# Opening stage of a one-core attention and gated-MLP kernel: last keys of the first step copied within SBUF, weights for the key bound fetched in two transfers on SP, and three pieces of work put elsewhere

## Chip, cores and metric

The kernel runs on one core of a Trainium2 chip. The metric is the device time of one execution in microseconds (us), the median of three runs of the kernel before: 1417.37, from 1417.25 to 1418.29.

## What is computed

The input x is 2048 x 512. A gate weighs two branches, an attention of 32 heads (16 columns each) and a gated MLP of width 1792:

```python
g = sigmoid(sum(x * gate_w, axis=-1))
q, k, v = split(x @ wqkv)               # 32 heads of 16
a = softmax(q @ k.T / 4) @ v @ wo       # each head over 2048 keys
b = (silu(x @ w1) * (x @ w3)) @ w2
out = g * a + (1 - g) * b
```

## The kernel before

Every fp32 product is made from three matmuls: a value is split into a high part (H, h, `hi`) and a low part (L, l, `lo`), and high by high, low by high and high by low are summed in PSUM.

**The opening stage** is written out by hand and ends where the first score matmul starts. It works on x in four blocks of 512 rows (0 to 3), and on V in tiles of 128 rows:

- `load_x(b)` (L116 to L120, on SP's queue) fetches a block. `transpose_x(b)` (L149): PE transposes it (L157), ACT copies the high part out of PSUM (xH, L160), DVE subtracts the low part (xL, L161).
- `project_qk(0, b)` (L176) makes queries and keys of the first eight heads for a block: 24 matmuls (L183), then ACT copies `hi` (L187), DVE subtracts `lo` (L188), and `store_qk` (L174, SP) writes them to four tensors in HBM, `kH_d`, `kL_d`, `qH_d`, `qL_d`. Inside the one of block 0, block 1 is transposed.
- `load_v` (L194) fetches V's weights in four pieces of 256 KB (L198, SP) that POOL splits (L200 and L201). They share fetch buffers with each other, so a fetch waits for the split of the one ahead. `project_v(t)` sums a tile of V (L97, L98, L99) in one of three PSUM banks, and ACT copies it out (L212).
- The scores have a bound that lets the kernel skip the search for row maxima. `squares` (L220) squares the query and key weights (ACT L223, sums on DVE L224), eight pieces in all. The first two are those that are projected with anyway; the six others come in six transfers that ACT issues (`load_w`, L124). `x_squares(b)` (L165, ACT) sums the squares of x's rows. `bound` (L226) takes their maxima (DVE L228, PE L231 and L232, DVE L233 to L235) and writes a flag (L236).
- `guard_rows` (L238) makes two rows per head that stand beside the queries and are subtracted in the score matmul (PE L241, DVE L242 to L246), and stores them in `m_d` (L248, SP, 256 KB each).
- `load_q` (L264), `load_k` (L257) and `load_guard` (L269) fetch from HBM what the first score step needs: `Qt` and `Kt`, 50 rows for each of two heads. The last quarter of the keys, those of block 3, is fetched after `project_qk(0, 3)` has stored it, by SP for the first head of the pair and by ACT for the second.
- `x_gate(b)` (L169, DVE) sums the gate's products; after block 3 the gate is finished (L385 to L388). `load_weights` (L323) fetches the first chunk of weights for the filling matmuls, split on POOL.
- `row_maxima` (L278) reads the flag on every engine (L280) and branches (L281). With these inputs the branch's body is skipped.

V tiles 7, 8 and 9 are summed on PE ahead of the branch, and copied out by DVE behind it (L397).

**The main loop** has 1024 units: a score matmul (L768), an exponential on ACT (L772) and a product with V (L756), with half-array matmuls of the projections and of the MLP between them. An order written out as a table sets what fills which unit. The next step's queries and keys are fetched after the seventh unit.

**What sets the order.** Each engine runs its instructions in the order in which they are written. SP and ACT issue the transfers used here. A transfer reports its landing on one of eight completion counters (DMAHW0 to DMAHW7), which are taken in turn, over all queues together. Before a transfer is issued, the one before it on its counter has landed. Behind a skipped branch, SP waits for each counter and adds what the body would have added, and the first score matmul waits for all eight.

Of the kernel before, what the change touches and what calls it, by code (L numbers as in the profile page):

```python
# [8 lines left out]
F32 = mybir.dt.float32  # L9
# [8 lines left out]
P = 128  # L18
S = 2048
D = 512  # L20
F = 1792
H = 32
DH = 16
NB = S // 512
NT = S // P
ND = D // P
# [8 lines left out]
def gated_mix_kernel(ctx: ExitStack, tc: tile.TileContext, x, wqkv, wo, w1, w3, w2, gate_w, out):  # L35
# [18 lines left out]
    nc = tc.nc  # L54
# [13 lines left out]
    sqp = ph1.enter_context(tc.tile_pool(name="sqp", bufs=1))  # L68

    QD = [[dram.tile([D, S], F32, name=f"{n}{p}_d") for p in "HL"] for n in "qk"]  # L70
# [40 lines left out]
    Kt = [qkp.tile([P, S], F32R, name=f"Kt{i}") for i in range(2)]  # L111
# [3 lines left out]
    def load_x(b):  # L115
        xn[b] = p1.tile([P, 4, D], F32, name="xn", bufs=2)  # L116
        src = x[512 * b:512 * b + 512, :].rearrange("(t p) d -> p t d", p=P)
        for t in range(0, 4, 1 if b < 2 else 4):
            e = t + (1 if b < 2 else 4)
            nc.sync.dma_start(xn[b][:, t:e, :], src[:, t:e, :])  # L120

    def load_w(c, tile=None, e=nc.sync):
        w = tile if tile is not None else slot("fr", F32, (P, ND, P))
        e.dma_start(w, wqkv[:, c:c + P].rearrange("(k p) n -> p k n", p=P))  # L124
        return w

    def split_w(w):
# [21 lines left out]
    def transpose_x(b):  # L149
        xH[b] = xp.tile([P, ND, 512], F32R, name=f"xH{b}")  # L150
        xL[b] = xp.tile([P, ND, 512], F32R, name=f"xL{b}")
        parts = ((0, 1, bank()), (1, 1, bank()), (2, 2, psum2()))
        for t in range(4):
            for k0, n, ps in parts:
                for k in range(n):
                    o = ps[:, P * t:P * t + P] if n == 1 else ps[:, k, P * t:P * t + P]
                    nc.tensor.transpose(o, xn[b][:, t, P * (k0 + k):P * (k0 + k) + P], ident)  # L157
        for k0, n, ps in parts:
            ps = ps if n == 2 else ps[:, None, :]
            nc.scalar.activation(xH[b][:, k0:k0 + n, :], ps, AF.Copy)  # L160
            nc.vector.tensor_sub(xL[b][:, k0:k0 + n, :], ps, xH[b][:, k0:k0 + n, :])  # L161

    def x_squares(b):
        for t in range(4):
            nc.scalar.activation(slot("sg", F32), xn[b][:, t, :], AF.Square, accum_out=x2[:, 4 * b + t:4 * b + t + 1])  # L165

    def x_gate(b):
        for t in range(4):
            nc.vector.scalar_tensor_tensor(slot("hx", F32), xn[b][:, t, :], 1.0, gw, op0=OP.mult, op1=OP.mult,  # L169
                                           accum_out=z[:, 4 * b + t:4 * b + t + 1])  # L170
# [2 lines left out]
        for t, d in zip((hi, lo), QD[i]):  # L173
            nc.sync.dma_start(d[P * c:P * c + P, 512 * b:512 * b + 512], t.bitcast(F32) if t.dtype == F32R else t)  # L174

    def project_qk(c, b, w, between=None):  # L176
        ps = psum2()
        for i in range(2):
            if i and between:
                between()  # L180
            for n, (h, xs) in enumerate(((0, xH), (0, xL), (1, xH))):
                for k in range(ND):
                    nc.tensor.matmul(ps[:, i, :], w[i][h][:, k, :], xs[b][:, k, :], start=n == k == 0,  # L183
                                     stop=n == 2 and k == ND - 1)
        hi = p1.tile([P, 2, 512], F32R, name="hi", bufs=2)
        lo = p1.tile([P, 2, 512], F32R, name="lo", bufs=2)
        nc.scalar.activation(hi, ps, AF.Copy)  # L187
        nc.vector.tensor_sub(lo, ps, hi)  # L188
        for i in (1, 0):
            store_qk(i, c, b, hi[:, i, :], lo[:, i, :])  # L190

    wv = []

    def load_v():  # L194
        for k in range(ND):
            n = "13"[k % 2]
            r = slot("fr", F32)
            nc.sync.dma_start(r, wqkv[P * k:P * k + P, 2 * D:3 * D])  # L198
            vh, vl = slot("fh" + n), slot("fl" + n)
            nc.gpsimd.tensor_copy(vh, r)  # L200
            nc.gpsimd.tensor_sub(vl, r, vh)  # L201
            wv.append((vh, vl))

    def sums_v(t):
        ps = bank()
# [5 lines left out]
    def project_v(t):  # L211
        nc.scalar.activation(*sums_v(t), AF.Copy)  # L212
# [7 lines left out]
    def squares(w, n):  # L220

        sq = slot("raw", F32, (P, ND, P))
        nc.scalar.activation(sq, w, AF.Square)  # L223
        nc.vector.tensor_reduce(rs[:, n, :], sq.rearrange("p k (h d) -> p h k d", d=DH), axis=AX.XY, op=OP.add)  # L224
# [13 lines left out]
    def guard_rows():  # L238
        ps = bank()
        one = V[0:1, 0, :, DH:DH + 1].rearrange("p h o -> p (h o)")  # L240
        nc.tensor.matmul(ps[0:H, 0:1], one, top[:, 2:3], start=True, stop=True)  # L241
        nc.vector.tensor_copy(mm, ps[0:H, 0:1])  # L242
        ones = V[0:H, :, :, DH:DH + 1].rearrange("p t h o -> p (t h o)")
        r = [slot("sg", F32R, (H, 512)) for _ in range(2)]
        nc.vector.tensor_scalar(r[0], ones, mm, None, op0=OP.mult)
        nc.vector.tensor_scalar(r[1], r[0], -1.0, mm, op0=OP.mult, op1=OP.add)  # L246
        for a in range(2):
            nc.sync.dma_start(M_d[:, a, :].rearrange("h (j t) -> h j t", t=512),  # L248
                              r[a][:].bitcast(F32)[:, None, :].to_broadcast([H, 4, 512]))

    def load_k(j, i, b0=0, b1=NB, e=(nc.sync, nc.sync)):
        c = slice(512 * b0, 512 * b1)
        for h in range(2):
            r = 64 * h
            s = slice(DH * (2 * j + h), DH * (2 * j + h) + DH)
            for o, ks in enumerate((0, 0, 1)):
                e[h].dma_start(Kt[i][r + DH * o:r + DH * o + DH, c].bitcast(F32), QD[1][ks][s, c])  # L257

    def load_q(j, half, i):
        for h in range(2):  # L260
            r = 64 * h
            s = slice(DH * (2 * j + h), DH * (2 * j + h) + DH)
            for o, qs in enumerate((0, 1, 0)):
                nc.sync.dma_start(Qt[i][r + DH * o:r + DH * o + DH, :].bitcast(F32),  # L264
                                  QD[0][qs][s, 1024 * half:1024 * half + 1024])

    def load_guard(j, half, i):
        for h in range(2):
            nc.sync.dma_start(Qt[i][64 * h + 48:64 * h + 50, :].bitcast(F32),  # L269
                              M_d[2 * j + h, :, 1024 * half:1024 * half + 1024])  # L270
# [48 lines left out]
    def load_weights(chunk):  # L319
        out = []  # L320
        for n, w in zip("13", chunk["src"]):
            r = slot("fr", F32, (P, ND, P))
            nc.sync.dma_start(r, w.rearrange("(k p) n -> p k n", p=P))  # L323
            if chunk["first"]:
                wh = slot("raw", F32R, (P, ND, P))
                wl = slot("raw" if n == "1" else "gw", F32R, (P, ND, P))
                split(wh, wl, r)
            else:
                wh = slot("fh" + n, F32R, (P, ND, P))
                wl = slot("fl" + n, F32R, (P, ND, P))  # L330
                splits.append((issued + 6, lambda a=(wh, wl, r): split(*a)))
            out.append((wh, wl))
        chunk["w"] = out

    chunks = [dict(src=(wqkv[:, P * c:P * c + P], wqkv[:, D + P * c:D + P * c + P]), first=c == 1)
              for c in range(1, ND)]
# [11 lines left out]
    wq = [split_w(w) for w in w0]  # L348
    for i in range(2):
        squares(w0[i], ND * i)  # L350
    ws = [(ND * i + c, load_w(i * D + P * c, sqp.tile([P, ND, P], F32, name=f"s{i}{c}"), nc.scalar))
          for i in range(2) for c in range(1, ND)]
    load_v()
    project_qk(0, 0, wq, lambda: transpose_x(1))
    x_squares(0)
    x_gate(0)
    load_x(2)
    project_qk(0, 1, wq)
    x_squares(1)
    x_gate(1)  # L360
    load_x(3)
    project_v(0)
    for n, w in ws[:ND - 1]:
        squares(w, n)
    project_v(1)
    for n, w in ws[ND - 1:]:
        squares(w, n)
    project_v(2)
    transpose_x(2)
    fill_k()  # L370
    project_v(3)
    x_squares(2)
    x_squares(3)
    project_qk(0, 2, wq)
    project_v(4)
    bound()
    transpose_x(3)
    guard_rows()
    x_gate(2)
    project_v(5)  # L380
    load_q(0, 0, 0)
    load_k(0, 0, 0, 3)
    load_guard(0, 0, 0)
    x_gate(3)
    nc.scalar.activation(g, z, AF.Exp, scale=-1.0)  # L385
    nc.vector.tensor_scalar(g, g, 1.0, None, op0=OP.add)
    nc.vector.reciprocal(g, g)
    nc.vector.tensor_scalar(omg, g, -1.0, 1.0, op0=OP.mult, op1=OP.add)  # L388
    load_weights(chunks[0])
    project_qk(0, 3, wq)  # L390
    load_k(0, 0, 3, NB, (nc.sync, nc.scalar))
    project_v(6)

    last_v = [sums_v(t) for t in range(7, EARLY_V)]
    row_maxima()
    for to, src in last_v:
        nc.vector.tensor_copy(to, src)  # L397
    ph1.close()
# [423 lines left out]
    k = ND - 1  # L822
# [14 lines left out]
    for t in range(NT // 2, NT):  # L837
        n, r = divmod(t - NT // 2, 2)
# [20 lines left out]
    for b in (2, 3):  # L859
        o, r = orr[b - 2]  # L860
# [34 lines left out]
```

## Time and profile before

| | us |
|---|---|
| median of three runs | 1417.37 |
| lowest and highest run | 1417.25, 1418.29 |
| the profiled execution | 1417.44 |
| its span, from the first to the last instruction | 1415.7 |
| PE (TensorE) busy | 1400.2 (99%) |
| ACT (ScalarE) busy | 1028.9 (73%) |
| DVE (VectorE) busy | 487.0 (34%) |
| POOL (GpSimd) busy | 319.5 (23%) |

The mean granted TensorE clock is 0.996 of full speed. The span leaves out 1.74 us around the first and the last instruction. PE's row counts matmuls; PEld is its weight loads, which run beside them. Times in timelines count from the start of the span. A row of DMA issues (SPq, ACTq) gives the time from the first issue's start to the last one's end, waits between them included.

### The profile page before, as it was taken

The page shows a single profiled execution, that of the slowest core. Times are in us where ns is not written, and L with a number is a line of the kernel's source. Part 1 is how long each engine was busy: PE and PEld are TensorE (multiplying, and loading weights), DVE is VectorE, ACT ScalarE, POOL GpSimd, SP SyncE. Part 2 cuts the span into 40 slices and gives each one's busy share as a digit, 9 for nine tenths or more (in the row PEclk, how much of TensorE's full clock was granted, in tenths as well). Part 3 has the DMA queues.
Part 4 walks back from the last instruction along what each step waited for, and adds up shares of the span by engine and source line. Part 5 has one row for each costly group of instructions (what it writes and reads, how often), then busy time and mean ns, then how long its engine had stood idle before and what let it go on. Part 6 is the DMA issues. An engine that isn't in the chain of part 4 may idle for free.

```text
span 1415.7 us, 29018 instructions
## 1 busy us (share of the span) xinstructions
PE 1400.2 (99%) x11471; PEld 833.0 (59%) x11471; DVE 487.0 (34%) x1079; ACT 1028.9 (73%) x1147; POOL 319.5 (23%) x356
## 2 busy tenths in 40 slices
PE   8999999999999999999999999999999999999998
PEld 6765565665655656656556556566555555555556
DVE  5501111254545455454555545541010110110113
ACT  4457776777777777777777777777688788878880
POOL 4201444211100110011011021643324332232240
PEclk9999999999999999999999999999999999999999
DMA  7623454533312333223232522544433342354434
GB/s 241 145 49 64 135 136 131 122 92 75 76 53 63 105 77 76 63 80 83 57 77 71 116 78 66 147 105 114 121 91 94 102 107 62 76 133 110 97 125 177
DMA packets 112863, 141.44 MB, mean 100 GB/s; under 512 B 16496, under 2 KB 70768, under 8 KB 109744
## 3 DMA queue, kind: packets, MB, share of 16 engines
q1 hardware_dynamic: 107312, 134.04, 38.1%
q10 hardware_dynamic: 5408, 5.47, 1.2%
q8 instruction: 92, 1.51, 0.5%
q14 instruction: 51, 0.42, 0.1%
HBM read 90.70 MB, written 48.76 MB: 99 GB/s over the span
## 4 chain that ended last, share of the span: by engine, by line
PE 94%; ACT 0%; DVE 0%; issue 0%; ACTq 0%
PE acc L756 33%; PE f L414 27%; PE S L768 19%; PE f L544 11%; PE f L630 1%; PE f L423 1%; PE f L97 0%; PE f L98 0%; PE f L99 0%; PE S L99 0%; PE S L98 0%; PE S L97 0%; ACT p L772 0%; PE acc L99 0%; PE acc L98 0%; PE acc L97 0%
## 5 line engine op out<-in xcount | busy, mean ns | idle before, releaser
L772 ACT ACTIVATE p<-S 128x1024 f32<-128x1024 f32 x1024 | 967.1, 1025 | 313.9 <-PE S L768 305.8
L756 PE MATMUL acc<-p,V 128*17 128x512 f32 x4096 | 472.1, 594 | 0.0
L768 PE MATMUL S<-Qt,Kt 50*128 50x512 f32 x2048 | 408.8, 410 | 0.9 <-PEq L281 0.6
L768 PEld LDWEIGHTS S<-Qt,Kt 50*128 50x128 f32 x2048 | 184.7, 184 | 175.8 <-issue 77.8
L756 PEld LDWEIGHTS acc<-p,V 128*17 128x17 f32 x4096 | 103.6, 97 | 276.4 <-issue 274.6
L457 DVE RECIPROCAL sg<-sg 128x64 f32<-128x64 f32 x448 | 209.5, 517 | 51.8 <-issue 49.7
L414 PE MATMUL f<-xL,fh 64*128 64x512 f32 x1024 | 206.0, 391 | 0.0
L414 PE MATMUL f<-xH,fh 64*128 64x512 f32 x1024 | 205.9, 390 | 0.0
L414 PE MATMUL f<-xH,fl 64*128 64x512 f32 x1024 | 205.5, 390 | 0.0
L316 POOL CAST fh<-fr 128x512 fp32r<-128x512 f32 x32 | 20.0, 626 | 436.5 <-DMA fr<-in_B_w_dram 425.7
L414 PEld LDWEIGHTS f<-xH,fh 64*128 64x128 f32 x1024 | 99.7, 186 | 21.8 <-DVE tick L729 0.4
L414 PEld LDWEIGHTS f<-xL,fh 64*128 64x128 f32 x1024 | 100.1, 187 | 20.9
L414 PEld LDWEIGHTS f<-xH,fl 64*128 64x128 f32 x1024 | 99.0, 184 | 20.2
L729 DVE MEMSET tick<- 1x1 f32 x196 | 11.6, 59 | 283.1 <-PE f L544 157.2
L544 PE MATMUL f<-xH,fl 64*128 64x512 f32 x208 | 61.8, 390 | 0.0
L544 PE MATMUL f<-xL,fh 64*128 64x512 f32 x208 | 60.9, 391 | 0.0
L544 PE MATMUL f<-xH,fh 64*128 64x512 f32 x208 | 59.8, 391 | 0.0
L449 DVE COPY gs<-f 128x512 f32<-128x512 f32 x56 | 38.7, 691 | 60.8 <-PE f L414 59.5
L544 PE MATMUL f<-xH,raw 64*128 64x512 f32 x192 | 56.1, 391 | 0.0
L737 DVE COPY u<-acc 128x512 f32<-128x512 f32 x32 | 22.1, 691 | 96.6 <-PE acc L756 93.6
L455 DVE TENSOR_SCALAR sg<-sg 128x512 f32<-128x512 f32 x56 | 26.2, 467 | 82.4 <-ACT sg L454 80.3
L563 DVE SCALAR_TENSOR_TENSOR y<-f,omg,y 128x512 f32<-128x512 f32 x32 | 24.0, 751 | 78.2 <-PE f L544 78.2
(231 smaller groups left out, 1366.2 us busy)
## 6 DMA issues: line engine op xcount, KB each, us to landing
Kt<-kH_d SPq DMA_DIRECT2D x124, 128.0 KB
h_d<-sg SPq DMA_DIRECT2D x56, 256.0 KB
sg<-h_d SPq DMA_DIRECT2D x43, 256.0 KB
fr<-in_B_w_dram SPq DMA_DIRECT2D x42, 256.0 KB
Qt<-qH_d SPq DMA_DIRECT2D x128, 64.0 KB
Kt<-kL_d SPq DMA_DIRECT2D x62, 128.0 KB
Qt<-qL_d SPq DMA_DIRECT2D x64, 64.0 KB
b_d<-y SPq DMA_DIRECT2D x16, 256.0 KB
```

The lines of the kernel that those rows point to most:

```text
L316: nc.gpsimd.tensor_copy(hi, src)
L414: return nc.tensor.matmul(ps, w[i == 2][r, k, :], (xL if i == 1 else xH)[b][r, k, :], start=n == 0 and not second, stop=n == 3 * ND - 1 an ...
L423: return nc.tensor.matmul(ps, (xL if i == 2 else xH)[b][r, k, o:o + P], wv[k][i == 1][r, :], start=n == 0 and not second, stop=n == 3 * ND ...
L449: nc.vector.tensor_copy(gs, ps)
L455: small.append(lambda: nc.vector.tensor_scalar(sg, sg, 1.0, None, op0=OP.add))
L457: small.append(lambda q=q: nc.vector.reciprocal(sg[:, q:q + 64], sg[:, q:q + 64]))
L544: ins = nc.tensor.matmul(ps, hs[t][q][i == 2][r, P * o:P * o + P], (w2L if i == 1 else w2H)[q][r, o, :], start=n == 0 and not second, stop ...
L563: nc.vector.scalar_tensor_tensor(y, ps, omg[:, t:t + 1], y, op0=OP.mult, op1=OP.add)
L737: nc.vector.tensor_copy(u, acc)
L756: nc.tensor.matmul(acc[r:r + DH + 1, :], V[:, k, 2 * j + h, :], p[:, h, :], start=k == 0, stop=k == NT - 1)
L768: nc.tensor.matmul(ps[:, h, :], Kt[i][r:r + 50, P * k:P * k + P], Qt[i][r:r + 50, t:t + 512], start=True, stop=True)
L772: nc.scalar.activation(p, ps, AF.Exp, scale=SCALE)
```

## The change

It has four parts:

- The six transfers for the bound, on ACT's queue, become two of 768 KB on SP's: `sk` (the key weights) between the second and the third of V's weights, `sq` (the query weights) after `load_x(2)`. The squares of `sk` stand after `project_v(0)`, those of `sq` after `project_v(3)`.
- The keys of block 3 are no longer fetched from HBM. `last_keys` copies them from `hi` and `lo` in SBUF into `Kt`, six transfers of 32 KB, issued by SP and ACT by turns, ahead of the stores of `hi` and `lo`.
- `load_q` and `load_k` for the first three blocks stand ahead of `guard_rows`.
- `x_gate(3)` and the gate's end stand behind `project_qk(0, 3)` and `project_v(6)`, and the first `load_weights` behind the branch.

The main loop is the same, its transfers too, but that the counters which they take are turned by four.

SP's instructions where V's weights are fetched, as a piece of the difference (fr are the fetch buffers, gw the gate's weights):

```order
 L138 DMA gw<-in_gate_w_dram 128x512
-L198 DMA fr<-in_A_wqkv_dram 128x512 x4
+L200 DMA fr<-in_A_wqkv_dram 128x512 x2
+L124 DMA sk<-in_A_wqkv_dram 128x4x384
+L200 DMA fr<-in_A_wqkv_dram 128x512 x2
 L174 DMA kH_d<-hi 128x512
 L174 DMA kL_d<-lo 128x512
```

One transfer of 768 KB now stands between the second and the third piece of V's weights.

ACT's instructions from V tile 2 to the `hi` of block 2, of before:

```order
L212 ACTIVATE V<-f 128x32x16
L160 ACTIVATE xH_427<-f 128x512 x2
L160 ACTIVATE xH_427<-S 128x1024
L212 ACTIVATE V<-f 128x32x16
L165 ACTIVATE sg,x_106<-xn 128x512 x8
L187 ACTIVATE hi<-S 128x1024
```

And of the change:

```order
L160 ACTIVATE xH_410<-f 128x512 x2
L160 ACTIVATE xH_410<-S 128x1024
L216 ACTIVATE V<-f 128x32x16
L227 ACTIVATE raw<-sq 128x512 x3
L165 ACTIVATE sg,x_106<-xn 128x512 x8
L187 ACTIVATE hi<-S 128x1024
```

Three squares of `sq` now stand between V tile 3 and the eight squares of x.

SP's instructions of the change around the guard stores and the keys of block 3, with the semaphores that each waits for (m_d are the guard rows, the counters' names end in _49):

```order
L267 DMA Kt_110<-kL_d 16x1536 [waits DMAHW5_49,Pool_49]
L252 DMA m_d<-sg 32x4x512 [waits DMAHW6_49,DVE_49]
L252 DMA m_d<-sg 32x4x512 [waits DMAHW7_49,DVE_49]
L279 DMA Qt_108<-m_d 2x1024 [waits DMAHW7_49,DMAHW6_49,DMAHW0_49]
L279 DMA Qt_108<-m_d 2x1024 [waits DMAHW1_49]
L259 DMA Kt_110<-hi 16x512 [waits DMAHW2_49,Activation_49]
L259 DMA Kt_110<-hi 16x512 [waits DMAHW3_49]
L259 DMA Kt_110<-lo 16x512 [waits DMAHW4_49,DVE_49]
L174 DMA kH_d<-hi 128x512 [waits DMAHW5_49]
L174 DMA kL_d<-lo 128x512
L174 DMA qH_d<-hi 128x512
L174 DMA qL_d<-lo 128x512 [waits DMAHW0_49]
```

And ACT's of the change at the same place:

```order
L187 ACTIVATE hi<-S 128x1024 [waits DMAHW6_49,DMAHW0_49,PE_49]
L259 DMA Kt_110<-hi 16x512 [waits DMAHW6_49,Activation_49]
L259 DMA Kt_110<-hi 16x512 [waits DMAHW7_49]
L259 DMA Kt_110<-lo 16x512 [waits DMAHW0_49,DVE_49]
L216 ACTIVATE V<-f 128x32x16 [waits PE_49]
```

The three copies that ACT issues use counters 6, 7 and 0. The values that SP's two guard stores wait for on 6 and 7 are those that stand when the first two of ACT's copies have landed. Before, the guard stores stood ahead of the fetches and waited on counters 3 and 4.

The diff:

```diff
@@ -119,9 +119,9 @@
             e = t + (1 if b < 2 else 4)
             nc.sync.dma_start(xn[b][:, t:e, :], src[:, t:e, :])
 
-    def load_w(c, tile=None, e=nc.sync):
+    def load_w(c, tile=None):
         w = tile if tile is not None else slot("fr", F32, (P, ND, P))
-        e.dma_start(w, wqkv[:, c:c + P].rearrange("(k p) n -> p k n", p=P))
+        nc.sync.dma_start(w, wqkv[:, c:c + w.shape[-1]].rearrange("(k p) n -> p k n", p=P))
         return w
 
     def split_w(w):
@@ -173,7 +173,7 @@
         for t, d in zip((hi, lo), QD[i]):
             nc.sync.dma_start(d[P * c:P * c + P, 512 * b:512 * b + 512], t.bitcast(F32) if t.dtype == F32R else t)
 
-    def project_qk(c, b, w, between=None):
+    def project_qk(c, b, w, between=None, direct=None):
         ps = psum2()
         for i in range(2):
             if i and between:
@@ -186,10 +186,12 @@
         lo = p1.tile([P, 2, 512], F32R, name="lo", bufs=2)
         nc.scalar.activation(hi, ps, AF.Copy)
         nc.vector.tensor_sub(lo, ps, hi)
+        if direct:
+            direct(hi[:, 1, :], lo[:, 1, :])
         for i in (1, 0):
             store_qk(i, c, b, hi[:, i, :], lo[:, i, :])
 
-    wv = []
+    wv, ws = [], []
 
     def load_v():
         for k in range(ND):
@@ -200,6 +202,8 @@
             nc.gpsimd.tensor_copy(vh, r)
             nc.gpsimd.tensor_sub(vl, r, vh)
             wv.append((vh, vl))
+            if k == 1:
+                ws.append(load_w(D + P, sqp.tile([P, ND, D - P], F32, name="sk")))
 
     def sums_v(t):
         ps = bank()
@@ -248,13 +252,19 @@
             nc.sync.dma_start(M_d[:, a, :].rearrange("h (j t) -> h j t", t=512),
                               r[a][:].bitcast(F32)[:, None, :].to_broadcast([H, 4, 512]))
 
-    def load_k(j, i, b0=0, b1=NB, e=(nc.sync, nc.sync)):
+    def last_keys(hi, lo):
+        for o, src in enumerate((hi, hi, lo)):
+            for h, e in enumerate((nc.sync, nc.scalar)):
+                r = 64 * h + DH * o
+                e.dma_start(Kt[0][r:r + DH, S - 512:S].bitcast(F32), src[DH * h:DH * h + DH, :].bitcast(F32))
+
+    def load_k(j, i, b0=0, b1=NB):
         c = slice(512 * b0, 512 * b1)
         for h in range(2):
             r = 64 * h
             s = slice(DH * (2 * j + h), DH * (2 * j + h) + DH)
             for o, ks in enumerate((0, 0, 1)):
-                e[h].dma_start(Kt[i][r + DH * o:r + DH * o + DH, c].bitcast(F32), QD[1][ks][s, c])
+                nc.sync.dma_start(Kt[i][r + DH * o:r + DH * o + DH, c].bitcast(F32), QD[1][ks][s, c])
 
     def load_q(j, half, i):
         for h in range(2):
@@ -348,51 +358,50 @@
     wq = [split_w(w) for w in w0]
     for i in range(2):
         squares(w0[i], ND * i)
-    ws = [(ND * i + c, load_w(i * D + P * c, sqp.tile([P, ND, P], F32, name=f"s{i}{c}"), nc.scalar))
-          for i in range(2) for c in range(1, ND)]
     load_v()
     project_qk(0, 0, wq, lambda: transpose_x(1))
     x_squares(0)
     x_gate(0)
     load_x(2)
+    ws.append(load_w(P, sqp.tile([P, ND, D - P], F32, name="sq")))
     project_qk(0, 1, wq)
     x_squares(1)
     x_gate(1)
     load_x(3)
     project_v(0)
-    for n, w in ws[:ND - 1]:
-        squares(w, n)
-    project_v(1)
-    for n, w in ws[ND - 1:]:
-        squares(w, n)
-    project_v(2)
+    for c in range(1, ND):
+        squares(ws[0][:, :, P * c - P:P * c], ND + c)
+    for t in range(1, 3):
+        project_v(t)
     transpose_x(2)
     fill_k()
     project_v(3)
+    for c in range(1, ND):
+        squares(ws[1][:, :, P * c - P:P * c], c)
     x_squares(2)
     x_squares(3)
     project_qk(0, 2, wq)
     project_v(4)
     bound()
     transpose_x(3)
+    load_q(0, 0, 0)
+    load_k(0, 0, 0, 3)
     guard_rows()
     x_gate(2)
     project_v(5)
-    load_q(0, 0, 0)
-    load_k(0, 0, 0, 3)
     load_guard(0, 0, 0)
+    project_qk(0, 3, wq, None, last_keys)
+    project_v(6)
     x_gate(3)
+
     nc.scalar.activation(g, z, AF.Exp, scale=-1.0)
     nc.vector.tensor_scalar(g, g, 1.0, None, op0=OP.add)
     nc.vector.reciprocal(g, g)
     nc.vector.tensor_scalar(omg, g, -1.0, 1.0, op0=OP.mult, op1=OP.add)
-    load_weights(chunks[0])
-    project_qk(0, 3, wq)
-    load_k(0, 0, 3, NB, (nc.sync, nc.scalar))
-    project_v(6)
 
     last_v = [sums_v(t) for t in range(7, EARLY_V)]
     row_maxima()
+    load_weights(chunks[0])
     for to, src in last_v:
         nc.vector.tensor_copy(to, src)
     ph1.close()
```

## Prediction

> **What bounds the kernel now.** First the page: the engines' busy time and the chain that ended last.
> ```profile
> span 1415.7 us, 29018 instructions
> PE 1400.2 (99%) x11471; PEld 833.0 (59%) x11471; DVE 487.0 (34%) x1079; ACT 1028.9 (73%) x1147; POOL 319.5 (23%) x356
> PE 94%; ACT 0%; DVE 0%; issue 0%; ACTq 0%
> ```
> TensorE is busy for all but 15.5 us, and the chain lies on it. The change touches nothing behind the first score matmul and takes no matmul away, so it can only move PE's pauses and its half-clock stretches in the opening stage. PE's timeline shows them (start, duration, in brackets the idle time before and its releaser).
> ```profile
> 20.76 1.51 PE L183 MATMUL S<-xH,wh 128*128 128x512 f32 x4 [4.55 <-DVE xL L161]
> 25.21 1.10 PE L183 MATMUL S<-xH,wh 128*128 128x512 f32 x4
> 28.00 0.40 PE L97 MATMUL f<-fh,xH 128*128 128x512 f32 x1
> 49.63 0.27 PE L232 MATMUL f<-ident,am 128*1 128x128 f32 x1
> 50.18 0.33 PE L157 MATMUL f<-ident,xn 128*128 128x128 f32 x1 [0.18 <-ACT V L212]
> 61.63 0.40 PE L97 MATMUL f<-fh,xH 128*128 128x512 f32 x1
> 73.33 0.79 PE L97 MATMUL f<-fh,xH 128*128 128x512 f32 x1 [3.15 <-ACT V L212]
> 79.44 0.93 PE L768 MATMUL S<-Qt,Kt 50*128 50x512 f32 x4 [0.62 <-PEq L281]
> ```
> There are two large pauses: 4.55 us ahead of block 1's projection, and 3.15 us ahead of the last V sums. Each is followed by a half clock, as the windows show (length, busy time of PE, PEld, DVE, ACT and POOL, granted clock, DMA share, GB/s).
> ```profile
> 16.20:20.80 4.60, 0.05 (x2) 0.04 (x1) 2.61 (x4) 3.35 (x6) 1.87 (x2) 1.00 0.33 104
> 20.80:25.20 4.40, 4.40 (x12) 3.49 (x13) 4.33 (x6) 1.99 (x8) 3.38 (x4) 0.61 0.72 245
> 73.30:79.40 6.10, 5.49 (x12) 3.80 (x12) 0.54 (x1) 0.00 (x0) 0.00 (x0) 0.50 0.28 48
> 79.40:86.60 7.20, 7.16 (x59) 6.29 (x63) 0.27 (x3) 6.30 (x7) 0.00 (x0) 0.99 0.67 141
> ```
> I divide the opening at E, the end of `project_qk(0, 3)` on PE (61.63, where the next V sum starts), and S, the first score matmul (79.44). From S on the execution takes 1336.3 us, and that stays.
>
> **Up to E: block 1 starts earlier.** ACT's and DVE's rows show what held it.
> ```profile
> 10.26 7.14 ACTq L124 DMA_DIRECT2D s<-in_A_wqkv_dram  x4
> 17.45 1.09 ACT L160 ACTIVATE xH<-f 128x512 fp32r<-128x512 f32 x2 [7.87 <-DMA fr<-in_A_wqkv_dram]
> 19.48 1.22 DVE L161 TENSOR_TENSOR xL<-S,xH 128x1024 fp32r<-128x1024 f32 x1
> 13.02 0.38 PE L157 MATMUL S<-ident,xn 128*128 128x128 f32 x2
> ```
> The transposes of block 1 are done about 13.2, but ACT is inside the last four of its six weight issues until 17.40. Without them xH starts some 4.3 us earlier, and the pause falls from 4.55 to about 0.25. A pause that short is followed by no slow clock: the 12 matmuls from 20.76 to 25.21 took 4.45, those from 25.21 to 28.00 took 2.79, so 1.65 more goes. Project V of block 0 then starts near 22.05, not 28.00: **−5.95**.
>
> **V's weights take part of it back.** All four share one POOL chain, and two now queue behind the 768 KB transfer for the squares.
> ```profile
> 12.32 1.27 POOL L201 TENSOR_TENSOR fl<-fr,fh 128x512 fp32r<-128x512 f32 x1
> 17.06 0.61 POOL L200 CAST fh<-fr 128x512 fp32r<-128x512 f32 x1 [3.47 <-DMA fr<-in_A_wqkv_dram]
> 17.75 1.26 POOL L201 TENSOR_TENSOR fl<-fr,fh 128x512 fp32r<-128x512 f32 x1
> 21.66 0.61 POOL L200 CAST fh<-fr 128x512 fp32r<-128x512 f32 x1 [2.64 <-DMA fr<-in_A_wqkv_dram]
> 25.05 1.62 POOL L201 TENSOR_TENSOR fl<-fr,fh 128x512 fp32r<-128x512 f32 x1
> ```
> The second weight arrived 3.47 after the first one's split, beside ACT's transfers; the third 2.64 after the second's. Now the second shares the DMA engines with one transfer issued behind it, and not with six ahead: I put its arrival at 16.2, an estimate between 2.65 and 3.4 behind its issue at 13.6 (its buffer is free when the first split ends, 12.32 + 1.27), and the end of its split 2.0 later, as the rows have it (17.06 to 19.01): 18.25. The third arrives 2.65 behind that, at 20.9. From there two splits come one behind the other, 3.9 at the pace of the second one, 5.0 at that of 21.66 to 26.67, which ran beside DVE's gate sums; those start 4 us earlier now and cover about half of it, so I take 4.4: the last low half is ready at 25.3. PE wants it after 10 matmuls of V (0.233 each, from 12 in 2.79), at 24.4. That is **+0.9**. Ends: 0 (no contention, the second landing in 2.65) and +2.1 (the split ends at 26.5, close to the old 26.67).
>
> **Squares later.** Three squares (1.67 together) move from ACT's slack at 32 to behind project V(3), ahead of x_squares and of block 2's `hi`.
> ```profile
> 32.05 1.67 ACT L223 ACTIVATE raw<-s 128x512 f32<-128x512 f32 x3
> 45.93 0.62 ACT L165 ACTIVATE sg<-xn 128x512 f32<-128x512 f32 x1
> 46.74 1.02 ACT L187 ACTIVATE hi<-S 128x1024 fp32r<-128x1024 f32 x1
> 48.94 0.16 DVE L228 TENSOR_REDUCE am<-x 128x1 f32<-128x16 f32 x1
> ```
> ACT runs eight squares of x without a gap into that `hi`, which PE's sums had been ready for only just before, so `hi`, `lo` and DVE's maximum shift by nearly 1.67 against PE. The maximum was done at 49.10 and PE took it up at 49.63, half a microsecond later: PE now waits about 1.25 there. The 0.18 of the stall at 50.18, with what PE loses at the transposes around it, 0.3 in all, lies inside that wait and goes: **+0.93**. Ends: 0 (ACT is ahead by then, because PE's own work shrank) and +1.25. E falls by 5.95 − 0.9 − 0.93 = **4.1**, to 57.5.
>
> **From E to S: what the key copies wait for.** In the order, the three copies that ACT issues take completion counters 6, 7 and 0, and take their turn ahead of SP's two guard stores. Those stores wait for counters 6 and 7, so for copies of keys that do not exist before E, though their rows lie ready from 56 on. Behind them on SP stand the two guard fetches (waiting for both stores), three copies, four stores, and the flag's read and branch. PE waits for none of this until S, whose ten waits include all eight counters, and these get their last increments from SP behind its branch.
> ```profile
> 28.20 1.02 ACT L187 ACTIVATE hi<-S 128x1024 fp32r<-128x1024 f32 x1 [5.41 <-PE S L183]
> 55.88 0.48 DVE L246 TENSOR_SCALAR sg<-sg,mm 32x512 fp32r<-32x512 f32 x1
> 55.80 0.89 SPq L248 DMA_DIRECT2D m_d<-sg  x2
> 49.89 0.44 SPq L174 DMA_DIRECT2D qL_d<-lo  x1
> 58.00:59.00 1.00, 1.00 (x6) 0.81 (x5) 0.97 (x3) 0.00 (x0) 0.00 (x0) 1.00 0.99 195
> 59.00:60.00 1.00, 1.00 (x6) 0.77 (x6) 0.93 (x4) 0.00 (x0) 0.00 (x0) 1.00 0.69 225
> 72.27 0.30 SPq L257 DMA_DIRECT2D Kt<-kL_d  x1
> L281 SPq EVENT_SEMAPHORE  x8: 17/17/17, 77.6 to 78.2; - x8
> L281 SPq COMPARE_BRANCH  x1: 50/50/50, 73.9 to 73.9; - x1
> ```
> Working from E: `hi` ends at E+1.2 (the block 1 copy: 28.20 against 28.00, 1.02 long), its copy is issued at E+1.3. A copy of 32 KB inside SBUF is in no row; the 256 KB fetch's 2.64 bounds it above, 1.5 is my lower end, an estimate without a row, and I take 2.0, nearer to the row that there is. First store E+3.25, second E+3.7. The old pair was issued from 55.80 to 56.69 and the DMA engines were full until 59 and 0.69 busy to 60, with fetches beside: 3 to 3.6 after the second issue; I take 3.6, E+7.3, as the copies are in flight beside them. Guard fetches and three copies at 0.3 to 0.45 each reach E+9.3; four stores at 0.46 E+11.1. From the last key issue's end (72.57) to the last increment at 78.2 took 5.63, of which 3.7 lay between branch and first increment and doesn't depend on the data: E+16.75. S follows 0.2 later, **E+16.95** against the old 17.81: **−0.9**.
>
> PE itself needs 48 matmuls of 0.233 and is done at E+11.4: it stands for some 5.4 us, longer than the 3.15 that gave the half clock of 73.3 to 79.4. So a half clock comes at the head of the main loop, where every us of it costs half. Before, it lay ahead of S (0.50, then 0.99 from 79.40) and is in the 17.81. Such stretches lasted 3.4 (0.61 over 4.40) and over 6.1 us; a part may pass before S, so 2.8 to 6.2 remain, 4.5 in the middle. Cost **+2.1** (1.3 to 2.9), less 0.1 that before paid too.
>
> [...]
>
> **Costed at nothing.** The gate sums of block 3 and the gate itself move behind the keys, and end before SP's branch. The chunk's weights, now behind the branch, are fetched near S and split in about 4 us on POOL, against a first use some 35 us behind S, as the group of PE's first matmuls of them shows:
> ```profile
> L414 PE MATMUL f<-xH,raw x10: 386/390/393, 114.2 to 117.5; 64*128 64x512 f32 x10
> ```
> The first V copies wait only on ACT's issues, done by E+3. If that cover fails, each costs what remains of its length, under 1 us. The V copies that DVE makes behind the branch wait for nothing new.
>
> **Sum**: 1417.44 − 4.1 − 0.9 + 2.0 = **1414.4**. The profiled execution (1417.44, 1.74 around its span) is 0.07 above the median. Its bounds: V's weights −0.9 to +1.2 about the value taken, the squares −0.93 to +0.3, the copy −0.5 to +0.65, the clock −0.8 to +0.8. All at their better ends give 1411.3, all at their worse 1417.4; as they are independent I take some two thirds of that, **1412.4 to 1416.2**.
>
> **Rivals.**
> 1. The stores are not held by the counters, or are issued early. Then SP is done before PE, S stands at E+11.9, and there is no slow clock: 57.5 + 11.9 = 69.4, S 10.0 earlier, **1407.4**. For it: guard rows ready long before E. Against: the order shows the wait.
> 2. The early gain is half lost, because the 768 KB transfer delays V's weights to the far end (+1.2 on what I took), and block 3's input, which queues behind the second such transfer, arrives late for its squares on ACT (+1.0, two of its eight squares of 0.62 at most being behind their data): **1416.6**. For it: DMA share 0.72 and 245 GB/s at 20.8 to 25.2. Against: the shares of 0.33 ahead of it.
> 3. Slower. The last stores land late and SP, whose counter waits behind the branch need every transfer landed, ends late.
> ```profile
> 65.00 0.44 SPq L174 DMA_DIRECT2D kH_d<-hi  x1
> 70.50 0.78 SPq L257 DMA_DIRECT2D Kt<-kH_d  x2
> ```
> The store of 65.00 released its fetch 5.5 us later, that of 65.55 at 72.27, 6.7. From an issue ending at E+11.1, a landing 8.5 later gives counters at E+20 and S at E+20.5: +2.7 rather than −0.9, so 1418.0, and with the longer clock stretch **1418.8**. It decides from the point where S is 19.9 behind E: then the gap eats all of the 4.1. Against: those stores ran beside twelve fetches and two weights; here only themselves.
>
> **How the numbers follow.** Forecast 0.70, rival 1 0.08, rival 2 0.14, rival 3 0.08. 0.2% (2.8 us, about what a measurement here tells from no change) lies at 1414.5 and 1420.2. Of the forecast's 0.70, 0.38 lies below 1414.5, its value being close to that bound: with rival 1 faster 0.46. The other 0.32, rival 2 and half of rival 3, which at 1418.8 is still inside, give 0.50 within; the half of rival 3 where landings are later still gives slower 0.04. The range takes in the forecast's bounds and rival 2 with 0.4 more, and below it half the way to rival 1's side: 1410.5 to 1417.0, with rival 1, rival 3 and a few of the forecast's worst cases outside.
>
> **What would show it.** Right: xH of block 1 at 13 and no pause over 0.5 us before it; clock 1.00 from 20 to 25; project V a few tenths late; L232 waiting on DVE; guard stores issued behind ACT's first copy; PE idle for 4 to 6 us ahead of S and clock 0.50 behind it. Wrong: guard stores issued ahead of E (rival 1), SP's counter wait behind the branch ended by a landing store (rival 3), or V's low half arriving at 26.5 (rival 2).

## Result and profile after

The changed kernel takes 1418.23 us (median of 12 runs, 1417.28 to 1419.82), the kernel before beside it 1417.38 (12 runs, 1416.46 to 1418.56): ratio 1.0007, interval 0.9998 to 1.0016. The forecast was 1414.4, in a range of 1410.5 to 1417.0. The profiled execution took 1419.40, 1.2 above its median, with a span of 1417.6.

PE's timeline of the changed kernel, the rows that answer to those of before:

```profile
12.62 0.38 PE L157 MATMUL f<-ident,xn 128*128 128x128 f32 x2
17.55 1.19 PE L183 MATMUL S<-xH,wh 128*128 128x512 f32 x4 [0.22 <-DVE xL L161]
23.25 0.40 PE L97 MATMUL f<-fh,xH 128*128 128x512 f32 x1
26.28 0.50 PE L98 MATMUL f<-fl,xH 128*128 128x512 f32 x1 [0.55 <-POOL fl L203]
47.50 0.27 PE L236 MATMUL f<-ident,am 128*1 128x128 f32 x1 [1.71 <-DVE am L232]
59.13 0.40 PE L97 MATMUL f<-fh,xH 128*128 128x512 f32 x1
79.55 1.42 PE L777 MATMUL S<-Qt,Kt 50*128 50x512 f32 x4 [9.07 <-SPq L291]
```

The pause of 4.55 us ahead of block 1 is down to 0.22, and the one of 3.15 ahead of the last V sums is gone. In their place stands one of 9.07, and its releaser is SP behind the branch. E is 59.13, S is 79.55: 20.42 apart, where it was 17.81.

Before, block 1's transposes began at 11.50, as PE's timeline of that kernel has it:

```profile
11.50 0.38 PE L157 MATMUL f<-ident,xn 128*128 128x128 f32 x2
```

Four stretches give the whole difference of the spans (1417.6 against 1415.7, +1.9): the start up to block 1's transposes, where PE's order has not changed (11.50 before, 12.62 now: +1.12); from there to E (50.13 before, 46.51 now: −3.62); E to S (+2.61); and from S on (1336.26 before, 1338.05 now: +1.79). The start of the profile of before was an early one: in the eleven experiments below, two of them with the old code up to there, the transposes begin at 12.2 to 12.7. So the sizes to hold against the prediction are the other three.

The windows of the changed kernel behind the pause and at the head of the loop (length, busy time of PE, PEld, DVE, ACT and POOL, granted clock, DMA share, GB/s):

```profile
76.00:79.40 3.40, 0.00 (x0) 0.00 (x0) 0.00 (x0) 0.00 (x0) 0.00 (x0) 0.50 0.03 11
79.50:86.70 7.20, 7.15 (x38) 7.04 (x39) 0.12 (x2) 4.10 (x5) 3.27 (x4) 0.60 0.63 167
```

The loop's first 7.2 us run at a clock of 0.60, and PE does 38 matmuls in them; before it was 59 at 0.99.

SP's issues of the changed kernel from the guard stores on:

```profile
62.45 0.92 SPq L252 DMA_DIRECT2D m_d<-sg  x2
66.51 0.58 SPq L279 DMA_DIRECT2D Qt<-m_d  x2
67.19 2.28 SPq L259 DMA_DIRECT2D Kt<-hi  x2
69.56 0.54 SPq L259 DMA_DIRECT2D Kt<-lo  x1
70.15 0.58 SPq L174 DMA_DIRECT2D kH_d<-hi  x1
70.78 0.43 SPq L174 DMA_DIRECT2D kL_d<-lo  x1
71.26 1.74 SPq L174 DMA_DIRECT2D qH_d<-hi  x1
73.05 0.43 SPq L174 DMA_DIRECT2D qL_d<-lo  x1
```

ACT's copies, and the groups of the branch's line (SP's eight increments behind it, and how long SP and PE stood in the branch itself; PE's branch is the row of PEldq, 3772 ns):

```profile
60.38 1.24 ACTq L259 DMA_DIRECT2D Kt<-hi  x2
```

```profile
L291 SPq EVENT_SEMAPHORE  x8: 17/17/17, 78.8 to 79.3; - x8
L291 SPq COMPARE_BRANCH  x1: 50/50/50, 75.0 to 75.0; - x1
L291 PEldq COMPARE_BRANCH  x1: 3772/3772/3772, 66.7 to 66.7; - x1
```

The guard stores go out at E+3.3, behind the copies that ACT issued from 60.38 on, though their rows were ready at 53.9 (DVE's L250). Two issues are long: the two copies of `hi` take 2.28 together, the store of `qH_d` 1.74.

### The profile page after: what moved, and what is told of

Read it like the earlier page. It is cut to its first block, busy times and chain, and to the rows that moved or that the text cites. A ratio compares the mean times of both kernels' runs of the same rounds, so it can differ in the third digit from the quotient of the medians.

```text
span 1417.6 us, 29022 instructions
## 1 busy us (share of the span) xinstructions
PE 1398.8 (99%) x11471; PEld 834.0 (59%) x11471; DVE 485.6 (34%) x1079; ACT 1029.0 (73%) x1147; POOL 318.2 (22%) x356
## 3 DMA queue, kind: packets, MB, share of 16 engines
q8 instruction: 92, 1.51, 0.5%
## 4 chain that ended last, share of the span: by engine, by line
PE 94%; ACT 0%; DVE 0%; issue 0%; ACTq 0%
PE acc L765 32%; PE f L423 27%; PE S L777 19%; PE f L553 11%; PE f L432 1%; PE f L639 1%; PE f L97 0%; PE f L98 0%; PE f L99 0%; PE S L98 0%; PE S L97 0%; PE S L99 0%; ACT p L781 0%; PE acc L98 0%; PE acc L97 0%; PE acc L99 0%
## 5 line engine op out<-in xcount | busy, mean ns | idle before, releaser
L326 POOL CAST fh<-fr 128x512 fp32r<-128x512 f32 x32 | 19.9, 623 | 434.7 <-DMA fr<-in_B_w_dram 424.5
```

The costliest lines, as they stand in the source:

```text
L326: nc.gpsimd.tensor_copy(hi, src)
```

## Experiments

Each ran beside the kernel before on the same chip; ratios are against it. The theory to start with: guard stores behind ACT's copies start SP's chain late; the chain sets S; the pause that it leaves on PE brings a half clock. The rivals: SP's list is too long in any order, or a landing sets S.

**All key copies on SP.** ACT then takes no counter.

```diff
-            for h, e in enumerate((nc.sync, nc.scalar)):
+            for h, e in enumerate((nc.sync, nc.sync)):
```

> The changed kernel, with all six key copies issued by SP, so that ACT takes no completion counter and the guard stores no longer wait for copies of keys. Theory (the counter wait starts SP's late chain): guard stores are issued before E, PE is done with its 48 sums before or about when SP is through, S stands 12 to 14 us behind E instead of 20.4, no half clock stands ahead of the loop: 1408 to 1411 us. Rival (SP has too much to issue behind E whatever the order, or the landing of the last stores decides): S stays 17 us or more behind E, 1415 or more.

Measured: 1414.31, ratio 0.9972 (0.9963 to 0.9982). SP's timeline:

```profile
56.20 0.84 SPq L252 DMA_DIRECT2D m_d<-sg  x2
61.07 2.52 SPq L259 DMA_DIRECT2D Kt<-hi  x4
66.49 0.46 SPq L174 DMA_DIRECT2D qL_d<-lo  x1
```

And PE's:

```profile
59.82 0.40 PE L97 MATMUL f<-fh,xH 128*128 128x512 f32 x1
74.36 1.42 PE L777 MATMUL S<-Qt,Kt 50*128 50x512 f32 x4 [3.19 <-SPq L291]
```

The guard stores go out 3.6 us ahead of E, so the wait for ACT's counters is shown. S stands 14.5 behind E, 5.9 less than in the changed kernel, but more than the 12 to 14 expected, and the time lies between the two expectations: PE still pauses 3.19, and from S on it takes 1338.04, as with the long pause. Both theories had a part: the counter wait costs most, and the list of issues and the branch behind it the rest.

**The early part alone**, on the kernel before: two transfers for the bound on SP and the squares as changed; the fetches, gate sums, first weights and key fetches as before.

```diff
-    ws = [(ND * i + c, load_w(i * D + P * c, sqp.tile([P, ND, P], F32, name=f"s{i}{c}"), nc.scalar))
-          for i in range(2) for c in range(1, ND)]
...
+                ws.append(load_w(D + P, sqp.tile([P, ND, D - P], F32, name="sk")))
...
+    ws.append(load_w(P, sqp.tile([P, ND, D - P], F32, name="sq")))
```

> The kernel before with the early part alone: the weights for the bound in two transfers on SP, squares as in the changed kernel, all else as before. Theory (the early part brings what it was costed at, and is lost later): E falls by about 3.5 us, the 17.8 us from E to S stay, 1413.3 to 1414.5 us. Rival (the early gain is lost already by late inputs and late V weights, because all of SP's transfers pile up): 1416 to 1418.

Measured: 1414.38, ratio 0.9973 (0.9963 to 0.9984). E is 59.00, S 76.05, and S to the end 1336.05. The early part brings 3.7 us by itself; the changed kernel gives it all back behind E. From E to S this profile has 17.05 rather than the 17.8 expected: the clock ahead of S was 0.65 and 0.69 here, not 0.50, behind a pause that is no shorter (3.27).

**The key copies alone**, on the kernel before, by turns on SP and ACT.

```diff
-    project_qk(0, 3, wq)
-    load_k(0, 0, 3, NB, (nc.sync, nc.scalar))
+    project_qk(0, 3, wq, None, last_keys)
```

> The kernel before with the key copies alone, issued by SP and ACT by turns as in the changed kernel; the order of the rest as before. In this order the copies that ACT issues take their counters ahead of the fetches of the first keys, so nearly all of SP's list waits for block 3. Theory (counter wait): S stands 18 to 22 us behind E, 1417.5 to 1422 us. Rival (copying within SBUF saves the way over HBM whatever the counters): S stands 13 to 14 us behind E, 1412 to 1414.

Measured: 1423.0, ratio 1.0031 (1.0018 to 1.0043). SP's timeline shows the first fetch of keys, for blocks 0 to 2, behind ACT's copies of block 3:

```profile
63.05 0.42 SPq L272 DMA_DIRECT2D Qt<-qH_d  x1
68.00 1.66 SPq L265 DMA_DIRECT2D Kt<-kH_d  x2
```

ACT issued its first copy at 66.04; SP's next fetch follows 1.96 later, after 4.5 us of standing. S is 21.3 behind E (64.29 and 85.60), with a pause of 9.96 on PE. So this half of the change, alone, makes the kernel slower by 5 us, a little more than expected.

**The key copies alone, all on SP.**

```diff
-            for h, e in enumerate((nc.sync, nc.scalar)):
+            for h, e in enumerate((nc.sync, nc.sync)):
```

> The kernel before with the key copies alone, all six issued by SP. Theory (without a counter taken by ACT, copying within SBUF saves the way over HBM): S stands 14 to 15 us behind E rather than 17.8, PE pauses 2.5 to 3.5 us ahead of S and pays up to 2.4 us of half clock for it: 1 to 3 us faster than the kernel before, ratio 0.998 to 0.9993. Rival (SP's list, with the weights and the stores behind the copies, is as long as the way over HBM): ratio 1.000 or more.

Measured: 1418.37, ratio 1.0001 (0.9992 to 1.0010): no gain. S is 16.6 behind E, later than expected, since SP was busy with its older fetches and the weights until E+3.4 and the last store took 1.61. What is left of the gain from E to S, about 1 us, is eaten by the half clock (0.57 from 78 to 82) behind a pause of 5.28: from S on it takes 1338.22. (The profiled execution, 1420.23, was the longest of this kernel's runs.)

**PE kept busy in the pause**, in the changed kernel: first with 150, then with 72 transposes without a use.

```diff
     row_maxima()
+    idle(72)
     load_weights(chunks[0])
```

> The changed kernel with 150 transposes without a use on PE between the branch and the first score matmul, so that PE doesn't stand still for 9 us. Theory (the half clock behind that pause costs 1.8 us in the loop): S stays where it is, the clock is at 1.00 behind it, 1416.0 to 1416.8 us. Rival (the loop starts slowly for another reason, such as the late fetches of weights): no change, 1418 to 1418.5; if the transposes hold S up, more.

> The changed kernel with 72 transposes without a use (0.11 us each) on PE between the branch and the first score matmul, some 8 us that fit into PE's pause of 9. Theory (the half clock behind the pause costs 2.2 us in the loop's first ten units): S stays, the first ten units take what they took before, 2 us less than the changed kernel, ratio 0.9990 to 0.9995. Rival (the loop's slow start has another cause): ratio 1.0007 as in the changed kernel.

Measured: with 150 transposes 1428.53, ratio 1.0067 (1.0053 to 1.0081). They take 16.57 us, more than the pause of 9, and hold S up to 90.56; this run tells nothing of the total. The clock behind S is 1.00 there as well, but the loop takes 1337.54 from S on, 0.5 less than in the changed kernel: PE stands idle for 1.1 us between 80 and 160 us behind S, for a reason that was not followed up. With 72 the median is 1417.7, ratio 1.0000 (0.9991 to 1.0009). Windows of the run with 72, at the head of the loop:

```profile
80.40:87.60 7.20, 7.20 (x60) 5.81 (x63) 0.12 (x2) 6.54 (x8) 3.75 (x4) 1.00 0.87 197
```

The clock is at 1.00, PE does 60 matmuls instead of 38, and the loop takes 1335.43 from S on, 2.6 less than in the changed kernel, with S as far behind E as there (20.46). The weights come about as late in both, so the slow start is the clock. The ratio, 1.0000, misses the expected 0.9990 to 0.9995; against the 1.0007 of the changed kernel it goes the expected way, but the intervals overlap: the total shows the 2 us neither way.

**PE's branch later**: the same 72 transposes ahead of it.

```diff
+    idle(72)
     row_maxima()
     load_weights(chunks[0])
```

> The changed kernel with 72 transposes without a use on PE ahead of the branch, so that PE reaches its branch some 8 us later, when SP has issued its keys and stores, and the fetch of instructions behind that branch falls elsewhere. Theory (an issue of SP that falls into a fetch of instructions takes 1.3 to 1.7 us rather than 0.4 to 0.6): none of SP's three key copies and four stores takes over 0.7, the last is issued 11.5 to 12.3 us behind E rather than 14.4. Rival (the issues are long because the transfers themselves are slow to be taken): the same long issues, the second key copy and the third store. The time says little, since PE is held up on purpose: S about 19 to 21 behind E at full clock, ratio 0.999 to 1.001.

Measured: 1421.50, ratio 1.0025 (1.0015 to 1.0034). This is more than expected, since PE's branch now stands in the way: S is 22.4 behind E, and PE pauses 3.18 ahead of it; from S on it takes 1338.0, as the changed kernel does behind its half clock. What counts is SP's timeline, to be held against the one of the changed kernel above:

```profile
67.83 1.26 SPq L259 DMA_DIRECT2D Kt<-hi  x2
69.18 0.53 SPq L259 DMA_DIRECT2D Kt<-lo  x1
69.77 0.58 SPq L174 DMA_DIRECT2D kH_d<-hi  x1
70.39 0.44 SPq L174 DMA_DIRECT2D kL_d<-lo  x1
70.89 0.44 SPq L174 DMA_DIRECT2D qH_d<-hi  x1
71.37 0.44 SPq L174 DMA_DIRECT2D qL_d<-lo  x1
```

No issue takes over 0.7 (the two copies take 0.64 and 0.57 with a gap), and the last is through at E+12.05 (E is 59.76), against E+14.35. So 2.3 us of SP's lateness came from PE's branch. What it is about the branch is not shown by this. In the changed kernel the view of DMA queues has an instruction transfer of 16 KB (92 on that queue in the whole run, 1.51 MB) from 67.7 and one from 71.2, where the two long issues stand (1.58 from 67.9, 1.74 from 71.26):

```profile
q8 instruction: 1, 0.02, 5.7%
```

That row stands in the view of 67.70 to 69.20 and in that of 71.20 to 72.70, 1.0 and 4.5 us behind PE's branch of 66.7. In the run with the later branch, neither is there. The run with the key copies alone, by turns, has the pair again: PE's branch at 71.9, instruction transfers at 72.8 and 76.6, SP's two copies from 73.45 on taking 2.08 and its store of `kL_d` from 76.83 on 1.52.

**Stores of block 3 on POOL**, key copies on SP. POOL stands idle there (24.37 us ahead of its first store), and in the built order of this run its four stores report on DMASW0 to DMASW3, none of the eight counters of SP and ACT.

```diff
-            store_qk(i, c, b, hi[:, i, :], lo[:, i, :])
+            store_qk(i, c, b, hi[:, i, :], lo[:, i, :], nc.gpsimd if direct else nc.sync)
```

> The changed kernel with all six key copies on SP, as in the first run, and the four stores of block 3 issued by POOL, whose transfers take none of the eight counters. Theory (behind E, SP's number of issues and the branch behind them set S, and PE's pause there brings the half clock): SP is through some 2 us earlier than in the first run, S 12 to 13 us behind E, PE's pause under 1.5 us, no half clock, 4 us less than the first run: ratio 0.994 to 0.995, 1409 to 1410.5. Rival (the landing of the stores, or instruction fetches behind the branch, set S): S 14.5 us behind E as in the first run, ratio 0.9972.

Measured: 1410.87, ratio 0.9948 (0.9935 to 0.9962). PE's timeline:

```profile
60.08 0.40 PE L97 MATMUL f<-fh,xH 128*128 128x512 f32 x1
72.16 0.93 PE L777 MATMUL S<-Qt,Kt 50*128 50x512 f32 x4 [0.72 <-DVE V L406]
```

And the window at the loop's head:

```profile
72.20:79.40 7.20, 7.03 (x55) 6.24 (x55) 0.88 (x4) 6.13 (x7) 3.16 (x4) 1.00 0.63 166
```

S is 12.1 behind E, as expected. PE goes almost straight from its sums into the loop, its releaser is no longer SP, and the clock stays at 1.00. SP's eight increments end at 70.7, and PE is through its own branch at 71.5.

**The bound behind block 3's transposes**, in the changed kernel and on top of the stores on POOL.

```diff
-    bound()
     transpose_x(3)
+    bound()
```

> The changed kernel with bound() behind transpose_x(3), so that PE transposes block 3 while DVE's maximum, made late by the three squares, is still under way. Theory (the squares ahead of x_squares cost PE 1.2 to 1.7 us at the maximum, and in some executions a half clock behind it): 1.2 to 2 us less than the changed kernel, about 1416.5 where the kernel before has 1417.4, ratio 0.9985 to 0.9995. Rival (the late end is bound by SP's chain that does not hang on this): no change against the changed kernel, ratio 1.0007.

> The kernel with the stores of block 3 on POOL and the key copies on SP, and bound() behind transpose_x(3) as well. Theory: the two gains add up, 1.2 to 2 us less than without the move: ratio 0.993 to 0.994, 1407.5 to 1409. Rival (E comes earlier, but SP's chain doesn't, because the guard rows hang on the flag's maxima): as without the move of bound, 0.994 to 0.995.

Measured: 1422.48, ratio 1.0031 (1.0019 to 1.0043), and 1414.45, ratio 0.9976 (0.9966 to 0.9987): each about 4 us worse than without, where 1.2 to 2 us less had been expected. From the first one's timeline of PE:

```profile
51.05 0.27 PE L236 MATMUL f<-ident,am 128*1 128x128 f32 x1 [2.89 <-DVE am L232]
52.09 0.24 PE L245 MATMUL f<-top,V 1*32 1x1 f32 x2 [0.78 <-DVE top L239]
```

Its DVE and its window behind that place:

```profile
50.84 0.16 DVE L232 TENSOR_REDUCE am<-x 128x1 f32<-128x16 f32 x1
```

```profile
54.00:58.00 4.00, 4.00 (x14) 3.16 (x13) 2.58 (x8) 0.60 (x1) 0.00 (x0) 0.69 0.60 133
```

My theory looked at PE alone. In DVE's order the maximum also moved, behind block 3's low parts (xL, until 50.8), and PE waited 2.89 and 0.78 in place of 1.71. The clock then falls (0.69 from 54 to 58), which the changed kernel does not show there (1.00).

**The squares put otherwise on ACT**, on top of the stores on POOL.

```diff
+    x_squares(2)
+    for c in range(1, ND):
+        squares(ws[1][:, :, P * c - P:P * c], c)
     project_v(3)
-    for c in range(1, ND):
-        squares(ws[1][:, :, P * c - P:P * c], c)
-    x_squares(2)
-    x_squares(3)
     project_qk(0, 2, wq)
+    x_squares(3)
```

> The kernel with the stores of block 3 on POOL and the key copies on SP (ratio 0.9948 before), and the squares put otherwise on ACT: those of block 2 of x and of the query weights ahead of V tile 3's copy, those of block 3 of x behind the high part of block 2. Theory (the wait of PE for the maximum, 1.4 to 1.7 us, is the squares ahead of that high part): the wait is about 0.5 to 1.0 us, ratio 0.9940 to 0.9950, the fastest of all. Rival (block 3 of x lands so late that the maximum can't come earlier): the same wait, 0.9948 or a little more.

Measured: 1409.97, ratio 0.9944 (0.9930 to 0.9957), the fastest of all. From PE's timeline:

```profile
47.21 0.27 PE L236 MATMUL f<-ident,am 128*1 128x128 f32 x1 [0.77 <-DVE am L232]
```

The wait is 0.77 where the run with the stores on POOL had 1.37. In time the two cannot be told apart.

## Why the prediction was wrong

- **Up to E** it was right in kind and nearly in size. Block 1's projection lost its pause and the slow clock (1.00 from 14 to 28): from the transposes to project V it is 5.87 us shorter (5.95 forecast). V's weights cost a stall of 0.55 (0.9 with its bounds 0 to 2.1), the squares one of 1.71 at the maximum. The latter was too small in the sum (+0.93; the 1.25 behind it should have been 1.14 by its own rows, 1.67 − 0.53): ACT also waited for block 3 of x,

```profile
42.64 0.63 ACT L165 ACTIVATE sg<-xn 128x512 f32<-128x512 f32 x1 [0.81 <-DMA xn<-in_A_x_dram]
```

  which had been put among the rivals, as an input that queues behind the second transfer. Together E came 3.62 earlier (4.1 forecast), and the run with this part alone is faster by 3.7. That the profile comes so near is in part luck: in seven of the nine experiments with the changed early part PE also waits 0.3 to 1.5 for block 2 of x, ahead of its transposes near 33, which the forecast did not have and the profile of the changed kernel does not show. In the five experiments whose order differs from the changed kernel's only behind E, the stretch up to E takes 47.5 to 50.2, not 46.5.
- **The counter wait** was right, and to within 0.1 us: `hi` done at E+1.2, the guard stores at E+3.3, both landed and the first guard fetch issued at E+7.4, as worked out. No row of before shows the 2.0 for the copy within SBUF: it had been picked between a bound from another row (2.64) and a value without a row (1.5). In the changed kernel 2.07 lie between ACT's first issue (60.38) and the store that waits for it (62.45); that it came out is luck.
- **From E to S is the step that failed**: "−0.9", S at E+16.95, measured +2.6, S at E+20.42. The mechanism was right, and the term mis-sized is SP's seven issues between the guard fetches and the branch: three copies and four stores "reach E+11.1", and were through at E+14.35. I priced them from rows of other transfers. A copy within SBUF took 0.53 to 0.64 to issue with the later branch rather than 0.3 to 0.45, and two of the seven, which stand beside the fetches of instructions behind PE's early branch, took over 1.5 (1.58 and 1.74). The later branch shows the division: 0.95 of the 3.25 for the plain prices, 2.3 for PE's branch, which the sum had at nothing. Before, PE stood in its pause of 3.15 and reached its branch at 74.0, when SP's issues for S were done, so the opening of before does not show the two together. Its loop does: there is an instruction transfer at 82.6, and of two like pairs of fetches the one issued next takes 1.1 longer:

```profile
81.49 0.87 SPq L257 DMA_DIRECT2D Kt<-kH_d  x2
82.87 1.96 SPq L257 DMA_DIRECT2D Kt<-kH_d  x2
```

  The forecast could have been warned by that row. The 5.6 from the last issue to the last increment was right (5.8).
- **The half clock** was right: "+2.0" in all, 1.79 from the spans, and taken away by the transposes (2.6 against them). PE's pause was 9.07, not the 5.4 forecast, but the price did not grow with it: behind 3.19, with all key copies on SP, the loop takes as long (1338.04 against 1338.05).
- **Rivals.** The first (stores not held) is refuted. The third named the point from which the change loses, S 19.9 behind E, and the gap passed it, but not by its cause: SP's 3.8 us from the branch to the first increment are those of before (3.7), and the view of SP's waits names no landing there, only its own branch (3.7). The DMA engines were all but idle from 76.0 on (share 0.03 up to 79.4), and the first increment came at 78.8. The second holds in part, by the 0.81.
- From E to S the sum is off by 3.5 us, up to E by 0.5, at the clock by −0.2: 1414.4 with these is 1418.2, against 1418.23. That it closes so well is chance too, since the profile of before had an early start and that of the changed kernel lies 1.2 above its median.

What stays open: why, and whether, it is the fetch of instructions behind PE's branch that holds up SP's issues. The runs show that the long issues go when the branch goes, and that fetches and long issues come together. That blocks 2 and 3 of x land late because of the transfers for the bound was not tried by itself.

## What to carry to other kernels

When transfers share completion counters in turn, look up in the built order which transfer holds each counter ahead of a waiting one: a copy issued by another engine can stand ahead of stores that were ready long before, and moving the issue to the queue that waits anyway, or to one with counters of its own, was worth more here than the copy itself (3.9 and 4.6 us for the key copies on SP, 3.4 for the stores on POOL, against nothing). Work taken off one engine's path is only worth something if the next wait is not as late; here 3.7 us of gain needed the key copies on SP and the stores on POOL to become 7. A pause on the matmul engine cost twice here, once by itself and once by the clock behind it. The second cost was about 2 us behind a pause of 3.19 as behind one of 9.07, and the clock stayed at 1.00 behind one of 0.72, so the last microseconds of these pauses were the dear ones.

## What the hardware showed beyond that

- Pauses of nearly the same length did not always lower the clock. In the changed kernel the clock stayed at 1.00 from 46 to 58 with a pause of 1.71 us ahead of L236; in the run with 150 transposes, the same program up to there, 1.87 us at that place gave these windows:

```profile
50.00:54.00 4.00, 3.43 (x14) 2.72 (x13) 2.32 (x3) 2.00 (x3) 0.00 (x0) 0.50 0.93 210
54.00:58.00 4.00, 4.00 (x14) 3.15 (x14) 3.75 (x11) 0.60 (x1) 0.00 (x0) 0.72 0.56 142
```

  and E came at 62.6 rather than 59.1. With PE's later branch the pause there was 1.90, and the clock stayed at 1.00 from 46 to 58. What decides it was not shown, nor whether it is why the changed kernel's runs spread over 2.5 us.
- The skipped branch cost PE 3.35 to 5.27 us in these runs and SP, from the branch to the first increment, 2.7 to 5.1. It is not a matter of both branching at once: in the kernel before they do, at 73.9 and 74.0, and it cost 3.35 and 3.7. What went with it for SP was the traffic: in the 2.5 us behind SP's branch the DMA share was 0.73 to 0.78 in the three runs with 4.5 to 5.1 (all key copies on SP, the bound moved in the changed kernel, the later branch), and 0.12 to 0.44 in the ten others, with 2.7 to 3.9. PE's 5.27 is the run with all key copies on SP, at a share of 0.99. No run varied the traffic by itself, and that the traffic is the cause was not shown. PE's branch showed in another engine's issues too: of SP's three copies and four stores two took 1.58 and 1.74 in the changed kernel, where a transfer of 16 KB came 1.0 us behind PE's branch and another 4.5 us behind it; with the later branch none took over 0.64.
- The copy of 32 KB within SBUF took 0.6 us to issue and was there about 2.0 after its start: ACT's was issued at 60.38, and the store that waits for it went out at 62.45.
